# Earlier folds, loaded taps, a finer last batch, and 33 unread products at the start of a fused attention and MLP kernel

## The chip, the cores and the metric

The kernel runs on one core of a Trainium2 chip. The metric is the device time of one execution in microseconds. Before the change it is 587.71 us, the median of three runs (587.62 to 588.37).

## What is computed

Eight batches of attention with packed queries, a gated layer and a gated MLP, all in float32 accuracy. Some weights arrive in float64.

```python
p_packed = sm_attn(p, k, v)              # 32 packed queries per head, 576 keys
out = sm_attn(q, p_packed, p_packed)     # 576 queries, 32 packed keys
x = ...                                  # (8, 576, 512), heads side by side
gate_pre[:, t] = sum over k of conv_w[k] * x[:, t - 4 + k]      # 5 taps
x = (sigmoid(gate_pre) * (x @ w_val)) @ moe_w_out
h = relu(x @ w_in)                       # 512 -> 1024
u, v = h[..., :512], h[..., 512:]
v_n = layer_norm(v)
v_s = einsum('ts,bsd->btd', w_spatial, v_n) + b_spatial
out = (u * v_s) @ moe2_w_out
```

## The kernel before, in words

**Products.** TensorE multiplies in pieces: a matrix is split into a high part (ScalarE, L138) and the rest (VectorE, L140), and a product is the sum of high times high, high times low and low times high. `mm3` and `mms` (L142 to L147) issue these as passes of 288 columns (512 for hv) at L144; nearly all of TensorE's time is there. PSUM tiles come from the pool `ps2`, which has four buffers.

**Setup.** Two of the weight matrices are multiplied once: moe_w_out times w_in gives `wp`, split in high and low parts. `load_raw` (L583) loads a chunk of 128 rows, 64 bits a number; `unit` (L588) decodes it by `from_f64` (L545): two ScalarE passes (L548, L553), a shift (L554) and a sum (L556) on VectorE. `fold` (L594) multiplies: for each of four column blocks m and each half of w_in (u, and v, which the order calls w) four products over k, 128x512 in full float32, two passes each, 32 products in all; then a copy of the high part (L608) and a subtraction (L610), each 128x512. `tap_rows` (L651 to L674) spreads the five convolution taps over the rows in which the first batch wants them: a transpose, a copy, five products with a 0/1 matrix `sel`, a copy. `spatial` and `final` split the two remaining weights.

**Stages of a batch.** `Attn`: sa (scores of p with k by L194, maximum L202 to L214, exponents L219), tr (transposes of these, L229), av (L238, then pp L252), ppt (transpose of pp, L264), sb (scores of q, L273), sn (softmax over them, L286 to L304), sb2 (L306, L311 and the split of the probabilities), m (pp times w_val, L325), cv (gate). Batch 0 alone takes its gate by cx (L360): the taps times pp (ppk, L257) stand in for the convolution. `Mlp`: val (probabilities times m, times the gate), hv (v half, with the layer norm), hu (u half), sp (spatial product; L510 multiplies by u, then g is split by L138 and L140), out (L518 to L537: 48 passes for each of four column blocks, a copy at L535, a store at L537).

**Order.** A string `ORDER` (L21) lists steps, as `0sp2` for the stage sp of tile 2 in batch 0, or `fv1.2` for two steps of a fold; `run` executes the generators in that order, and this fixes the order on each engine's queue. SP issues all loads and stores.

Of the kernel before, what the change touches and what calls it, by code (L numbers as in the profile page):

```python
# [34 lines left out]
0out1 0cv2 0cv0 0out1.2 0cv3 1val2.2 0out3 0cv1 1val1 0out3 0cv0 1val3 1val2 0cv3 1val3 1val2 1val0.3 1val3 1val1.2
0out1 0lk1 0out3 1val2 1val3 1sa0 1val3 1hv2.2 1sa0.3 1tr0 1hv1.2 1hu3.2 1lq1 1hv0 1sa0 1hv1 1tr1 1hv2 1av1 1hv1 1av1
1hu3 0lv0 1hv2 1av0.2 1av1 1hv1.3 2lq0 1av0 1hv2.2 1hu0.2 1lq0 1hv2 1hv0 1hv3 1hv0 1hv4 1hu0 1hv0.2 1hv3 1hv0.2
1ppt0.2 1hv3.2 1hu1 1hv4.3 1sb0 1hv3.2 1hv4 1m0 1sn0 1hv3 1hu1 1sn0.2 1hu1 1hu2.2 1sn1 1m0 1hv4.3 1m0 1hv4.2 1sp0.2
1sn0 1sb20 1sn1.3 1sb21.3 0out0 1sb21 1hu2 1sb20.2 1sp3.2 1lv0 1sb21.2 1sp3.2 1sp2 1sp0.2 1sp3 1sb20.2 1sp1.3 1sb20
1xt0.2 1sp1 1lk1 1sp2 0out3 1sp2.2 1sp0 1xt1.2 1cv0 2val0 1sp1 2val0 1cv3 1sp2 1out2.2 1cv0 1out2.2 1cv2 1cv3 1lv1  # L40
1out0 1out1.2 1cv0 1cv1 1out3 1out0 1cv3 1out1 1out3.2 1cv1 2val0 2val1.2 2val2 1cv2 1cv1 2val1 1lp0 2val2 2val0.2
2val3.2 1cv2 2val2 2val1 1lk0 2val1 1out0.2 2sa0 2val3 2val2.2 2val3 2lq1 2val3 2hv0 2hv3 2hv0 2sa0.2 2hu1.2 2sa0
2hv0.2 2tr0 2sa0 2tr1 2hv3 2hu1 2hv0.2 2hv3 2hv0 2hu0 2hv2 2hv3.2 2av1.2 2hv3 2av0 2hv3 2hv2.3 2av1 2lv1 2av0.2 2hv1
2ppt0 2hv1.2 2ppt0 2hv1 2hu0 2sb0 2hv2 2sn0 2hv4 2hv2.2 2sn1 2hv4.3 2sn0 2hv1.2 2sn1 2hv4.3 2hu0 2hu2.2 2hv4 2sn1 2hv1
2hu2 2hu3.3 2hv4.2 2sp1.2 2sn0.2 2sp1 2sb20 1out1 2sp0.2 2sb20 2sp1 2lv0 2sb20.2 2sp1 2sn1 2sb21.2 2sp2.2 1out3
2sb21.3 2lk1 2sp0.3 2sb20.2 2sp2.2 2lk0 2sp3.3 2sp2 2xt0.2 2sp3.2 2m0.2 2xt1 2sb21 2xt1 2cv0 2m0 2out1 2cv3 2out1 2cv0
2out1 3val2 2cv2 2cv3 2out2 2out0 2cv1 2out2 3val0.2 2out1 2out2.2 2cv1 3val1 2cv2 2cv0 3val0 3lq1 2out0.2 3val2 2cv3
3val1 2cv1 3val1 2out3 2cv2 2out3 3val2 3val3.2 3val0.2 3val1 3sa0 3val3 3val1 3val2.2 3val3 2out3 3lq0 3val3 3hv0.2
3hv1 3sa0.3 3hv1 3hv0.3 3lk1 3hv1.2 3hv3 3sa0 3tr1 3hv4 3hv1.2 3tr0 3hv0.2 3hv1 3hv3 3hv2.2 3av0 3hv3.2 3hv2 3av1
3hu3.2 3hv3.2 3av0.2 3av1.2 3hv3 3ppt0 3hv4.2 3hu3 2out0 3hu1 3hu2 3hv4.2 3ppt0 3sb0 3sn1 3hu2 3hv4 3hv2.2 3hu0 3hv4.2  # L50
3lp0 3hv2 3sn1 3sn0 3hu1 3hu0 3sn1.2 3sn0.2 3hu1 3sn0 3hv2 3hv4.2 3sp1 3hu0 3sp1 3sb21.3 3sp0 3sp2 3sp1.2 3sb20.2 3sp1
3sb21 3lv1 3sp2 3sb21 3hu2 3sp3 3sp0 3sp3 3sb20 3sp2 3sb20.2 3sp2.2 3sp0.2 3xt0 5lp0 3xt0 3sp3.2 3lk0 3sp0 3sb20 3sp3
3m0.2 3xt1 3out0 3xt1 2out3 3out0 3cv0 3cv2 3out0 3out1.2 3sb21 3m0 4val0.2 3cv0.2 4val2 3cv3 3out1 3cv2 3cv1 3out2.2
3out3.2 3out0 3cv3 4val0 3cv3 4val0 4val2 3cv1 4val1.2 3cv2 4val2 3out2 3cv1 4val1 4val2 4val1 3out2 4val0 4val3 4lq1
4val3.3 4val1 4sa0 4val2 4val3 3out3 4hv0.2 4sa0 4hv3 4sa0 4hv3 4hu2.2 4hv4 4hv3 3lv0 4hv3.2 4sa0 4hv0 3out3 4hv3.2
4hv1 4hv0.3 4sa0 4hv0 4hu1 4tr0 4hu1 4hv4.3 4tr1 4av1 4hv1 4av0 4hu2 4hv4.2 4hv2 4hv1.3 4av0 4hv1.2 4av1.2 4av0 4lk0
4hu3 4hu0.2 4lv1 4hu1 4hv2 4hv4.3 4hv2.5 4ppt0 4lq0 4hu0 4ppt0 4hv4 4sp2 4sb0 3out1 4sn0 4sn1 4sn0.2 4hu3.2 4sn1.3
4sp1 4sb21 4sn0 4sb20 4sp2.2 4sp3 4sb21.2 4sp1 4sb20 4sp2 4sp1 4sp0.2 4sb21 4sp3 4sp1 4sp2 4sb20.2 4sb21 4sp0 4lk1
# [22 lines left out]
def packed_attention_gated_mlp(  # L81
# [64 lines left out]
    def mm3(out, steps):  # L146
        mms(out, [p for (ah, al), (bh, bl) in steps for p in ((ah, bh), (ah, bl), (al, bh))])  # L147
# [653 lines left out]
```

## Time and profile before

| what | value |
|---|---|
| median of three runs | 587.71 us (587.62 to 588.37) |
| the profiled execution's own time | 587.61 us |
| its span, first to last instruction | 585.84 us |
| TensorE busy | 570.2 us, 97% |
| VectorE busy | 442.8 us, 76% |
| ScalarE busy | 298.1 us, 51% |
| first product of val | 55.86 us |
| last pass of TensorE | ends at 581.9 us |

The span is 1.77 us shorter than the execution's own time, which also holds what lies around the instructions. TensorE's weight loads (PEld) overlap its passes. A mean granted clock of TensorE of 0.999 stands in the profile, but in the first 18 us it records nothing, and the duration of the weight loads tells the level there.

### The profile page before, as it was taken

How to read it: one execution, taken by the hardware profiler on the slowest of the kernel's cores; microseconds unless marked ns; L12 is line 12 of the kernel's file. 1: busy time of each engine (PE TensorE's matmuls, PEld its weight loads, DVE VectorE, ACT ScalarE, POOL GpSimd, SP SyncE). 2: the span in 40 equal slices, each digit the busy share in tenths (PEclk: the TensorE clock that was granted, in tenths of full speed). 3: DMA queues.
4: the chain of work that ended last, by engine and by line, in shares of the span. 5: the costliest groups of instructions: out<-in, count | busy, mean ns of one | idle time of the engine just before them, and what ended most of it. 6: DMA issues, size and time to landing. Idle time of an engine off the chain costs nothing.

```text
span 585.8 us, 12443 instructions
## 1 busy us (share of the span) xinstructions
PE 570.2 (97%) x5267; PEld 503.1 (86%) x5267; DVE 442.8 (76%) x847; ACT 298.1 (51%) x524; POOL 27.3 (5%) x51
## 2 busy tenths in 40 slices
PE   3998999999999999999999999999999999999997
PEld 2444889898899989898999989898999899998997
DVE  3697899996879867898759866997779968885330
ACT  4678665654435634654436553655446454453321
POOL 2000010000100010001000010001000010001000
PEclk9999999999999999999999999999999999999999
DMA  8965430053203150023300422013500300000012
GB/s 318 409 268 179 152 107 22 1 194 121 62 1 112 62 204 11 21 67 116 97 1 21 168 90 104 19 49 103 190 24 21 102 2 2 1 20 21 1 41 81
DMA packets 16615, 52.55 MB, mean 90 GB/s; under 512 B 1968, under 2 KB 2992, under 8 KB 16560
## 3 DMA queue, kind: packets, MB, share of 16 engines
q1 hardware_dynamic: 16560, 51.77, 25.0%
q8 instruction: 41, 0.67, 0.5%
q14 instruction: 14, 0.11, 0.1%
HBM read 42.32 MB, written 9.44 MB: 88 GB/s over the span
## 4 chain that ended last, share of the span: by engine, by line
PE 93%; DVE 4%; DMA 1%; ACT 1%; issue 0%; SPq 0%; DVEq 0%; ACTq 0%
PE ps L144 82%; PE ps L601 2%; PE ps L238 2%; PE ps L194 2%; PE ps L341 2%; PE ps L273 2%; PE ps L325 1%; DMA kq<-kT 1%; PE ps L360 1%; DVE wp L610 1%; DVE sT L286 0%; DVE sT L306 0%; DVE mx L202 0%; DVE sm L301 0%; DVE raw L556 0%
## 5 line engine op out<-in xcount | busy, mean ns | idle before, releaser
L144 PE MATMUL ps<-ws,vn 128*128 128x288 f32 (+1 forms) x896 | 122.1, 295 | 0.0
L144 PEld LDWEIGHTS ps<-ws,vn 128*128 128x128 f32 (+1 forms) x896 | 119.6, 188 | 2.4 <-issue 1.3
L144 PEld LDWEIGHTS ps<-g,wp 128*128 128x128 f32 x768 | 103.5, 188 | 5.0 <-issue 3.2
L144 PE MATMUL ps<-g,wp 128*128 128x288 f32 x768 | 107.3, 296 | 0.0
L144 PE MATMUL ps<-g,wo 128*128 128x288 f32 x768 | 105.9, 295 | 1.0 <-DVE g L140 1.0
L144 PEld LDWEIGHTS ps<-g,wo 128*128 128x128 f32 x768 | 102.9, 188 | 3.0 <-ACT x L349 1.3
L380 DVE SCALAR_TENSOR_TENSOR acc<-x,cw,acc 128x572 f32<-128x572 f32 (+1 forms) x112 | 90.0, 815 | 4.3 <-ACT acc L376 1.0
L144 PE MATMUL ps<-wp,g 128*128 128x512 f32 x384 | 91.9, 393 | 0.0
L144 PEld LDWEIGHTS ps<-wp,g 128*128 128x128 f32 x384 | 70.8, 188 | 16.5 <-issue 0.7
L138 ACT CAST g<-g 128x576 fp32r<-128x576 f32 x64 | 42.4, 675 | 56.7 <-DVE g L510 40.8
L140 DVE TENSOR_TENSOR g<-g,g 128x576 fp32r<-128x576 f32 x64 | 47.7, 751 | 6.5 <-ACT g L138 5.7
L457 POOL TENSOR_TENSOR rstd<-rstd,mhalf 128x1 f32<-128x1 f32 (+1 forms) x40 | 23.6, 593 | 522.2 <-DVE rstd L455 447.6
L138 ACT CAST vn<-vr 128x512 fp32r<-128x512 f32 (+1 forms) x40 | 24.6, 622 | 45.1 <-DVE vr L459 45.0
L510 DVE TENSOR_TENSOR g<-ps,u 128x576 f32<-128x576 f32 x32 | 23.8, 753 | 27.4 <-PE ps L144 26.9
L535 ACT COPY o<-ps 128x576 f32<-128x576 f32 x32 | 20.3, 635 | 35.7 <-PE ps L144 35.7
L144 PE MATMUL ps<-Ah,Mh 128*128 128x288 f32 x128 | 37.9, 296 | 0.0
L144 PE MATMUL ps<-Ah,Ml 128*128 128x288 f32 x128 | 37.8, 295 | 0.0
L144 PE MATMUL ps<-Al,Mh 128*128 128x288 f32 x128 | 37.8, 295 | 0.0
L439 ACT ACTIVATE vr<-ps 128x512 f32<-128x512 f32 x32 | 19.2, 602 | 34.9 <-PE ps L144 32.3
L140 DVE TENSOR_TENSOR vn<-vr,vn 128x512 fp32r<-128x512 f32 (+1 forms) x40 | 27.0, 684 | 13.1 <-ACT vn L138 12.9
L451 DVE BATCH_NORM_STATS2 st<-vr 128x6 f32<-128x512 f32 (+1 forms) x40 | 27.4, 685 | 11.7 <-ACT vr L439 9.0
L459 DVE TENSOR_SCALAR vr<-vr,mv,rstd 128x512 f32<-128x512 f32 (+1 forms) x40 | 21.2, 536 | 11.9 <-POOL rstd L457 11.8
(108 smaller groups left out, 680.4 us busy)
## 6 DMA issues: line engine op xcount, KB each, us to landing
v<-vT SPq DMA_DIRECT2D x16, 650.0 KB, 5.0
kq<-kT SPq DMA_DIRECT2D x16, 576.0 KB, 4.7
kq<-qT SPq DMA_DIRECT2D x16, 576.0 KB, 4.3
outT<-o SPq DMA_DIRECT2D x32, 288.0 KB, 2.5
raw<-w_in SPq DMA_DIRECT2D x8, 512.0 KB, 10.4
raw<-w_outT SPq DMA_DIRECT2D x4, 512.0 KB, 9.9
raw<-w_val SPq DMA_DIRECT2D x4, 512.0 KB, 10.3
raw<-w_out SPq DMA_DIRECT2D x4, 512.0 KB, 7.6
```

Of the source, the lines that this page charges most:

```text
L138: nc.scalar.copy(out=hi, in_=src)
L140: nc.vector.tensor_tensor(out=lo, in0=src, in1=f32(hi), op=ALU.subtract)
L144: nc.tensor.matmul(out, lhsT=a, rhs=b, start=(i == 0), stop=(i == len(pairs) - 1))
L194: nc.tensor.matmul(ps[g][NPK * qt:NPK * qt + NPK, h // 2, SQ * (h % 2):SQ * (h % 2) + SQ], lhsT=pT_, rhs=k[:, SQ * qt:SQ * qt + SQ], start ...
L238: nc.tensor.matmul(ps[NPK * h:NPK * h + NPK, :65], lhsT=aT[:, 9 * (h // 2) + 4 * (h % 2) + t, :], rhs=v[:, h, t, :], start=(t == 0), stop= ...
L380: nc.vector.scalar_tensor_tensor(out=acc[:, sft:], in0=x[:, :S - sft], scalar=cw[:, c, tap:tap + 1], in1=acc[:, sft:], op0=ALU.mult, op1=A ...
L439: nc.scalar.activation(out=vr, in_=ps, func=AF.Relu)
L451: nc.vector.bn_stats(st[:w], vr[:w])
L457: nc.gpsimd.tensor_tensor(out=rstd[:w], in0=rstd[:w], in1=mhalf[:w], op=ALU.pow)
L459: nc.vector.tensor_scalar(out=vr[:w], in0=vr[:w], scalar1=mv[:w, 0:1], scalar2=rstd[:w], op0=ALU.subtract, op1=ALU.mult,)
L510: nc.vector.tensor_tensor(out=halves(t), in0=ps[:, :, :SH], in1=halves(self.u.pop(c)), op=ALU.mult)
L535: nc.scalar.copy(out=halves(t), in_=ps[:, :, :SH])
```

## The change

- *Taps*: `tap_rows` no longer computes on TensorE. The host repeats the rows (`conv_r`), one load of 128x1280 words brings them, and `from_f64` decodes them in place.
- *Folds*: `fold(j, hf)` makes two column blocks m in one PSUM tile, so that four copies and four subtractions of 128x1024 stand where there were eight and eight of 128x512. The u half comes first.
- *Halves*: the first chunk of w_outT and of w_in are loaded and decoded in two halves; sa yields after two heads, when one tile of k is read; in the last batch hv, hu, sp and out may be interleaved by three passes, and out has a PSUM tile, a copy and a store for each half of 288 columns.
- *Products*: `warm` issues 33 products of the identity with itself (128x128, float32) into one PSUM tile that nothing reads: eight before the first half of sa, six before the second, nineteen before the first fold.
- *Order*: a new `ORDER` for everything.

```diff
+FIRST = ("o0", "w0")
-ik0 ip0 ik1 ic0 cw0.3 cb0 rw0 uw0 sa0 cb0 ro0 sa0 cb0 uw0 uo0.2 rw1 uw1 iv1 cb0 sa0 uw0 uo0 fv3 fv2 sa0 uw1.2 ro1
+ip0 ik0 ik1 ro0 uo0 wm0.8 sa0 wm0.6 sa0.3 uo0 ru0 ro0 uu0.3 uo0 wm0.19 fu0 iv0 ru1 iv1 uo0.3 sa0 tr0 sa0 tr1 fu1 av0.2
...
-    def mms(out, pairs):
-        for i, (a, b) in enumerate(pairs):
-            nc.tensor.matmul(out, lhsT=a, rhs=b, start=(i == 0), stop=(i == len(pairs) - 1))
+    def mms(out, n, pair, cut=False):
+        for i in range(n):
+            a, b = pair(i)
+            nc.tensor.matmul(out, lhsT=a, rhs=b, start=(i == 0), stop=(i == n - 1))
+            if cut and i % 3 == 2 and i < n - 1:
+                yield
...
         def out(self, e):
             ps = ps2.tile([P, 2, 512], F32, tag="ps2", name="ps2")
             cs = slice(P * e, P * e + P)
+            t = f_p.tile([P, S], F32, tag="f", name="o")
+            dst = outT[self.b, e]
             for n in range(2):
+                if self.cut and n:
+                    ps = ps2.tile([P, 2, 512], F32, tag="ps2", name="ps2")
...
+                if self.cut:
+                    nc.scalar.copy(out=t[:, ss], in_=ps[:, n, :SH])
+                    nc.sync.dma_start(out=dst[:, ss], in_=t[:, ss])
+            if not self.cut:
+                nc.scalar.copy(out=halves(t), in_=ps[:, :, :SH])
+                yield
+                nc.sync.dma_start(out=dst, in_=t)
...
     def unit(kind, k):
         raw = raws[kind, k].rearrange("p (n t) -> p n t", t=2)
-        return from_f64(lambda: homes[kind](k), raw, DM, *early)
+        for s in parts(kind, k):
+            yield from from_f64(lambda: homes[kind](k)[:, s], raw[:, s], s.stop - s.start, *early)
+            yield
...
+    def fold(j, hf):
+        ps = ps2.tile([P, 2, 512], F32, tag="ps2", name="ps2")
         hs = slice(hf * DM, (hf + 1) * DM)
         for k in range(NC):
+            for i in range(2):
+                m = 2 * j + i
+                nc.tensor.matmul(
+                    ps[:, i], lhsT=woT[:, k, P * m:P * m + P], rhs=homes["uw"[hf]](k),
+                    start=(k == 0), stop=(k == NC - 1),
+                )
+                yield
...
+        hi, lo = (w[:, 2 * j:2 * j + 2, hs] for w in wp)
+        yield from split(hi, lo, ps)
+
+    def warm(_):
+        ps = ps2.tile([P, 2, 512], F32, tag="ps2", name="ps2")
+        while True:
+            nc.tensor.matmul(ps[:, 0, :P], lhsT=ident, rhs=ident, start=True, stop=True)
+            yield
...
     def tap_rows():
...
+        block = vn_p.tile([P, 4 * n], I32, tag="vn1", name="taps")
+        raw, tmp = block[:, :2 * n].rearrange("p (n t) -> p n t", t=2), block[:, 2 * n:]
+        nc.sync.dma_start(out=raw, in_=words(conv_r))
+        yield
+        dst = block[:, :n]
+        cwr.append(dst.bitcast(F32).rearrange("p (a b) -> p a b", a=CONV))
+        yield from from_f64(lambda: dst, raw, n, tmp=tmp)
```

On TensorE, at the end of the first scores and up to sb, the order before was this (`ps_...` are PSUM tiles, `cw` the taps, `woT` and `winv` or `raw` the two factors of a fold, `aT` the transposed exponents):

```order
L194 MATMUL ps_136<-kq,pbd 32x144
L661 MATMUL ps_169<-ident,cw 20x128
L668 MATMUL ps_194<-cwt,sel 128x128 x5
L601 MATMUL ps_209<-winv,woT 128x512 x2
L601 MATMUL ps_226<-winv,woT 128x512 x2
L601 MATMUL ps_209<-winv,woT 128x512
L238 MATMUL ps_243<-v,aT 32x65 x20
L238 MATMUL ps_266<-v,aT 32x65 x20
L601 MATMUL ps_226<-winv,woT 128x512
L264 MATMUL ps_308<-ident,pp 128x128
```

The same place in the change:

```order
L208 MATMUL ps_134<-kq,pbd 32x144
L628 MATMUL ps_124<-ident 128x128 x19
L615 MATMUL ps_218<-raw,woT 128x512
L615 MATMUL ps_244<-raw,woT 128x512
L253 MATMUL ps_246<-v,aT 32x65 x20
L253 MATMUL ps_273<-v,aT 32x65 x20
L615 MATMUL ps_218<-raw,woT 128x512
L615 MATMUL ps_244<-raw,woT 128x512
L279 MATMUL ps_314<-ident,pp 128x128
L615 MATMUL ps_244<-raw,woT 128x512
```

The taps' six products are gone, nineteen of the unread ones stand in their place, and two folds instead of five stand ahead of av.

On VectorE, between the softmax of batch 0 and the last pieces of setup, the change has these instructions (`sT` are the probabilities of q, `taps` the new decode, `wp` the subtraction of a fold):

```order
L566 ISA raw<-raw,tmp 128x1024
L564 TENSOR_SCALAR taps<-taps 128x640
L322 TENSOR_TENSOR sT<-sT,sm_390 128x576
L566 ISA taps<-taps 128x1280
L564 TENSOR_SCALAR raw<-tmp 128x512
L322 TENSOR_TENSOR sT<-sT,sm_396 128x576
L272 TENSOR_TENSOR ppk<-taps,pp 128x320 x2
L566 ISA raw<-raw,tmp 128x1024
L327 STREAM_TRANSPOSE an<-sT 128x576
L145 TENSOR_TENSOR wp_445<-ps_359,wp_444 128x2x512
L327 STREAM_TRANSPOSE an<-sT 128x576
L145 TENSOR_TENSOR wp_445<-ps_381,wp_444 128x2x512
```

Before, ppk stood ahead of sn, and the subtractions were eight of 128x512 behind both `an`.

On TensorE behind the last sp (`g_...` are the four split products that out reads, the buffer numbers kept), the order before:

```order
L144 MATMUL ps2_6746<-ws1_624,vn1_749 128x288
L144 MATMUL ps2_6811<-g_6763,wo20_805 128x288 x2
L144 MATMUL ps2_6811<-g_6763,wo21_806 128x288
L144 MATMUL ps2_6811<-g_6803,wo20_805 128x288 x2
L144 MATMUL ps2_6811<-g_6803,wo21_806 128x288
```

and in the change, the last rows of a stretch that begins with twenty-four such passes on the other three g:

```order
L150 MATMUL ps2_6861<-g_6838,wo20_672 128x288 x2
L150 MATMUL ps2_6861<-g_6838,wo21_673 128x288
L150 MATMUL ps2_6861<-g_6836,wo20_672 128x288 x2
L150 MATMUL ps2_6861<-g_6836,wo21_673 128x288
L150 MATMUL ps2_6831<-g_6869,wo20_672 128x288 x2
```

Before, g_6803 is first read three passes behind the last sp; now g_6869, the one made last, comes after thirty. On VectorE the last instructions before (`g2_...` is a product with u, `g_...` its low part, `ps2_6746` the last sp) were these:

```order
L140 TENSOR_TENSOR g_6766<-g2_6744,g_6766 128x576
L510 TENSOR_TENSOR g2_6785<-ps2_6729,u_6637 128x576
L510 TENSOR_TENSOR g2_6801<-ps2_6746,u_6586 128x576
L140 TENSOR_TENSOR g_6803<-g2_6785,g_6803 128x576
L140 TENSOR_TENSOR g_6806<-g2_6801,g_6806 128x576
```

and in the change, where `ps2_6730` is the last sp:

```order
L517 TENSOR_TENSOR g2_6802<-ps2_6737,u_6599 128x576
L517 TENSOR_TENSOR g2_6824<-ps2_6675,u_6795 128x576
L145 TENSOR_TENSOR g_6838<-g2_6824,g_6838 128x576
L145 TENSOR_TENSOR g_6836<-g2_6802,g_6836 128x576
L517 TENSOR_TENSOR g2_6845<-ps2_6730,u_6721 128x576
L145 TENSOR_TENSOR g_6869<-g2_6845,g_6869 128x576
```

Before, the low part of g_6803 stood behind the last tile's product with u; now only the last tile's own low part does.

## Rows read from the trace of the kernel before

**Rows 1.** Part 1 of the page: busy time, share of the span and instructions of each engine.
```profile
PE 570.2 (97%) x5267; PEld 503.1 (86%) x5267; DVE 442.8 (76%) x847; ACT 298.1 (51%) x524; POOL 27.3 (5%) x51
```

**Rows 2.** Busy time by stretches: us, each engine's busy time (instructions), granted clock, DMA share, GB/s.
```profile
18.48:55.86 37.38, 35.49 (x349) 15.77 (x347) 29.39 (x60) 26.06 (x47) 0.00 (x0) 1.00 0.70 266
55.86:568.41 512.55, 512.55 (x4755) 469.48 (x4747) 402.89 (x762) 258.34 (x450) 23.62 (x40) 1.00 0.20 69
```

**Rows 3.** TensorE's waits over the span: us in total, times, longest.
```profile
PE ps L194 <- DMA pbd<-pT: 4.9, 1, 4.9
...
PE ps L144 <- DVE g L140: 1.0, 1, 1.0
```

**Rows 4.** TensorE's timeline, 0 to 62 us: start, duration, instruction, idle before.
```profile
4.89 1.22 PE L194 MATMUL ps<-kq,pbd 64*32 64x144 f32 x32 [4.89 <-DMA pbd<-pT]
...
9.91 2.46 PE L668 MATMUL ps<-cwt,sel 20*128 20x128 f32 x10 [0.77 <-ACT cwt L664]
14.04 6.75 PE L601 MATMUL ps<-winv,woT 128*128 128x512 f32 x10 [1.67 <-DVE woT L556]
20.72 1.35 PE L238 MATMUL ps<-v,aT 128*32 128x65 f32 x80
...
24.27 1.20 PE L273 MATMUL ps<-kq,ppT 64*32 64x288 f32 x32
...
39.51 5.31 PE L601 MATMUL ps<-raw,woT 128*128 128x512 f32 x12
46.67 1.12 PE L601 MATMUL ps<-raw,woT 128*128 128x512 f32 x2 [1.85 <-DVE wp L610]
47.72 2.68 PE L360 MATMUL ps<-an,ppk 32*64 32x288 f32 x80
```

**Rows 5.** Timeline of TensorE's weight loads, 13 to 22 us.
```profile
17.62 0.34 PEld L601 LDWEIGHTS ps<-winv,woT 128*128 128x128 f32 x1 [0.52 <-issue]
18.47 0.20 PEld L601 LDWEIGHTS ps<-winv,woT 128*128 128x128 f32 x1 [0.52 <-issue]
18.91 0.19 PEld L601 LDWEIGHTS ps<-winv,woT 128*128 128x128 f32 x1 [0.24 <-issue]
```

**Rows 6.** ScalarE's timeline, 6 to 18 us: the first exponents.
```profile
12.69 1.20 ACT L219 ACTIVATE a<-ps,nb 128x144 f32<-128x144 f32 x4 [0.52 <-DVE nb L214]
```

**Rows 7.** Groups by line and form, 0 to 62 us: busy us, mean ns of one, idle before.
```profile
L610 DVE TENSOR_TENSOR wp<-ps,wp 128x512 fp32r<-128x512 f32 x8 | 5.3, 683 | 1.6 <-ACT wp L608 1.6
...
L556 DVE CUSTOM_DVE_ANT_0 raw<-raw,tmp 128x1024 uint16<-128x1024 uint16 x4 | 2.7, 684 | 0.0
...
L369 ACT ACTIVATE gate<-ps 128x288 f32<-128x288 f32 x8 | 2.6, 422 | 0.0
...
L554 DVE TENSOR_SCALAR raw<-tmp 128x512 int32<-128x512 int32 x4 | 1.7, 415 | 0.5 <-ACT tmp L553 0.5
...
L301 DVE TENSOR_REDUCE sm<-sT 128x18 f32<-128x576 f32 x2 | 1.4, 721 | 0.0
...
L140 DVE TENSOR_TENSOR Ml<-ps,Mh 128x1024 fp32r<-128x1024 f32 x1 | 1.2, 1225 | 2.5 <-ACT Mh L138 2.5
L325 PE MATMUL ps<-wval,ppT 64*32 64x512 f32 x16 | 1.1, 601 | 0.0
```

**Rows 8.** Timeline, 567 to 586 us.
```profile
567.92 0.76 DVE L510 TENSOR_TENSOR g<-ps,u 128x576 f32<-128x576 f32 x1 [1.11 <-PE ps L144]
568.60 1.58 DVE L140 TENSOR_TENSOR g<-g,g 128x576 fp32r<-128x576 f32 x2
...
569.40 12.50 PE L144 MATMUL ps<-g,wo 128*128 128x288 f32 x92 [0.99 <-DVE g L140]
...
582.00 0.64 ACT L535 COPY o<-ps 128x576 f32<-128x576 f32 x1 [0.96 <-PE ps L144]
```

**Rows 9.** DMA traffic, 2 to 38 us.
```profile
DMA packets 4152, 14.11 MB, mean 392 GB/s; under 512 B 582, under 2 KB 838, under 8 KB 4149
```

**Rows 10.** DMA issues, 560 to 586 us: KB each, median us from issue to landing.
```profile
outT<-o SPq DMA_DIRECT2D x6, 288.0 KB, 2.1
```

More of the change, by code (lines that the diff above doesn't have):

```diff
@@ L140, in split, with mm3, pair @@
         nc.vector.tensor_tensor(out=lo, in0=src, in1=f32(hi), op=ALU.subtract)
-    def mms(out, pairs):
-        for i, (a, b) in enumerate(pairs):
-            nc.tensor.matmul(out, lhsT=a, rhs=b, start=(i == 0), stop=(i == len(pairs) - 1))
-    def mm3(out, steps):
-        mms(out, [p for (ah, al), (bh, bl) in steps for p in ((ah, bh), (ah, bl), (al, bh))])
+    def mms(out, n, pair, cut=False):
[4 more added lines that the diff above has]
+                yield
+    def mm3(out, n, step, cut=False):
+        def pair(i):
+            (ah, al), (bh, bl) = step(i // 3)
+            return ((ah, bh), (ah, bl), (al, bh))[i % 3]
+        return mms(out, 3 * n, pair, cut)
     vn = []
@@ L179, in __init__, with scores, head @@
             self.pp = self.ppk = self.x = None
-        def heads(self, lhsT, kind):
-            src = [kq_t.pop((kind, self.b, i)) for i in range(2)]
-            return [ps2.tile([P, 2, 512], F32, tag="ps2", name="ps2") for _ in range(2)], [
-                (g, h, lhsT[64 * g:64 * g + 64, NPK * h:NPK * h + NPK], src[h // 2][64 * g:64 * g + 64, h % 2])
-                for h in range(4)
+        def scores(self):
+            return [ps2.tile([P, 2, 512], F32, tag="ps2", name="ps2") for _ in range(2)]
+        def head(self, lhsT, kind, h):
+            src = kq_t[kind, self.b, h // 2]
+            return [
+                (g, lhsT[64 * g:64 * g + 64, NPK * h:NPK * h + NPK], src[64 * g:64 * g + 64, h % 2])
                 for g in range(2)
@@ L189, in sa @@
         def sa(self, _):
-            ps, heads = self.heads(pbd_t.pop(self.b), "k")
-            for i in range(0, 8, 2):
+            ps = self.scores()
+            for h in range(4):
                 for qt in range(4):
-                    for g, h, pT_, k in heads[i:i + 2]:
+                    for g, pT_, k in self.head(pbd_t[self.b], "k", h):
                         nc.tensor.matmul(
@@ L269, in sb @@
         def sb(self, _):
[L270 removed]
+            ps = self.scores()
             for n in range(2):
[L272 to L277 removed]
+                for h in range(4):
+                    for g, pT_, q in self.head(self.ppT, "q", h):
+                        nc.tensor.matmul(
+                            ps[g][NPK * h:NPK * h + NPK, n, :SH],
+                            lhsT=pT_, rhs=q[:, n * SH:(n + 1) * SH],
+                            start=True, stop=True, tile_position=(64 * g, NPK * h),
+                        )
             self.sps = ps
@@ L400, in val @@
                 ss = slice(n * SH, (n + 1) * SH)
[L401 to L406 removed]
+                yield from mm3(
+                    ps[:, n, :SH], 2,
+                    lambda g: ((at.M[0][:, g, cs], at.M[1][:, g, cs]), (at.A[g][0][:, ss], at.A[g][1][:, ss])),
                 )
@@ L440, in hv @@
             else:
-                mms(ps, [(self.tail[:, k, :], wk) for k in range(NC) for wk in (w_hi[k], w_lo[k])])
+                yield from mms(ps, 2 * NC, lambda i: (self.tail[:, i // 2, :], (w_hi, w_lo)[i % 2][i // 2]))
                 yield
@@ L770, in by_pair @@
         return np.moveaxis(w, 0, axis)
+    conv = rows(by_pair(inputs["moe_conv_w"].T, 0)).transpose(1, 0, 2)
     wt, bias = inputs["moe2_w_spatial"].T, inputs["moe2_b_spatial"]
```

250 lines of the change are left out of this document (100 added, 150 removed).

## The prediction

> **What bounds the kernel now.** I read the views in this order. The page says that TensorE is busy for 97% of the span and VectorE for 76% [rows 1], but a share mixes stages, so the table of stretches comes next [rows 2]. From 55.86 to 568.41 us TensorE is busy 512.55 of 512.55 us: only fewer passes could shorten that stretch, and the change takes none away there. What an edit of order can win lies ahead of 55.86, where the first product of val starts, and behind 568.41. TensorE's waits, six in all, say how much: 4.9 us for p is the first, 1.0 for a g the last [rows 3], and the larger ones between are 1.7 for woT and 1.85 for a wp [rows 4]. Last come the timelines of the two ends [rows 4 to 8]. In front, S, the end of L273's products, is 25.47 us (24.27 + 1.20), and from there the chain of waits runs over VectorE up to the fold that starts at 46.67. Behind, TensorE ends at 581.9, and one copy and one store close the span at 585.84.
>
> The sum is made against the profiled execution, whose own time is 587.61. It is 0.1 us (0.02%) under the median of the three runs, 587.71, so nothing is added for that.
>
> **Taps.** The transpose, the wait for its copy (0.77 us) and the five products (2.46 us in ten passes [rows 4]) leave TensorE between 8.75 and 12.37; two ScalarE copies go too. Behind them the first fold waited 1.67 us for woT anyway [rows 4], so by itself their going saves nothing. In their place stand one load of 655 KB and one decode. The load is the 22nd on SP's queue; one chunk of w_in and all of w_val wait behind it, 1.7 us at the 392 GB/s of this stretch [rows 9], and are read long after they land. The decode adds a shift and a sum on VectorE, about 0.4 and 0.75 us from start to start, being 640 wide where the others are 512. Its two ScalarE passes stand against the two copies.
>
> **Up to S.** Before, five fold products (ten passes, 6.75 us) stand between the taps and av. Their weight loads are 0.34 us long and 0.85 apart for two passes until 17.62, and 0.20 long and 0.43 apart from 18.47 [rows 5]: the lower level of TensorE's clock (1.2 GHz), then the higher (2.4), after 4.4 us of folds without a gap. In the change two fold products stand ahead of av and three more before sb. Worked forward: p and the first k land near 5.0 as before, and the scores of two heads take 1.2; the second k lands near 7.4; the scores end at T = 9.3 (8.82 before). From T to the first exponent before took 3.9 us (to 12.69 [rows 6]) with two shifts of a decode in it; without them 3.2. Behind nb VectorE has the shifts and sums of half of woT and of the first u, 1.65 us: the first fold can start at 14.15. Two folds take 1.7 us at the higher clock; exponents (1.2 us a half [rows 6]) and transposes are done at 15.6 and 16.35, so av (1.35) ends at 17.2; two folds, 18.9; pp is ready at 19.05, ppt ends at 19.4, one fold at 20.3, sb at S = 21.5, 4.0 us earlier.
>
> **From S to val.** TensorE has 27 fold products left at 0.86 us (twelve passes in 5.31 us, two to a product [rows 4]), 23.2 us; cx takes 2 x 2.68 and m 1.09 [rows 4, 7]: 29.6 us. VectorE's list from sn's first transpose to Ml, each at the distance at which its kind follows another: 12 shifts at 0.34 and 12 sums at 0.60 (busy 0.42 and 0.68 [rows 7], overlapping), half a sum 0.35, the taps' 1.15, the softmax 9.0 (twelve wide instructions at about 0.7, as L301, and small ones), ppk 0.95, three subtractions of wp and Ml at 1.2, two of Al at 0.67: 29.0 us. A subtraction for two m at once costs 1225 ns where two single ones cost 2 x 683 = 1366 [rows 7], so 0.14 us goes for each pair. The two engines are even, and neither can hide the other's gaps. Before, VectorE waited 1.6 us for ScalarE's copies ahead of the eight L610 [rows 7]; for four I allow 0.7 us, since a copy is twice as wide. First val at S + 30.3 = 51.8 instead of 55.86: **-4.1 us.** Bounds: without gaps 51.1 (-4.8); with twice the allowance 52.5, and with another wait like TensorE's 1.85 on a wp [rows 4] 53.4 (-2.5).
>
> **The 33 products.** They are 66 passes in TensorE's queue, ahead of work that cannot pass them: eight products in the wait for p, six between the halves of the scores, nineteen in the wait for the first woT and u. The nearest row is L668 [rows 4]: ten passes of 128 columns, 0.21 us from start to start (2.46 less the last pass's own length), at the lower clock; 0.107 at the higher. The eight take 3.4 us from about 1.5 and are done near 5.0: hidden. The six take 1.3 or 2.6 us from 6.4, to between 7.7 and 9.0, against k at 7.4; that is the 0.5 us in T. The nineteen take 4.1 or 8.1 us against the 4.85 from T to the first fold: hidden at the higher clock, 3.3 over at the lower. Before, the clock rose 4.4 us after folds without a gap began; here TensorE works almost without one from 1.5 on, so I take the higher clock for the nineteen, and nothing beyond T. With the cover gone, the 66 would cost between 7.1 and 14.1 us. What they return is already in S: at the lower clock the first two folds would take 3.4 us instead of 1.7, and av would start at 17.6 instead of 16.35.
>
> **The middle.** From the first val to the last sp the same passes stand in another order, 0.136 us each whichever stage they are of (92 in 12.50 [rows 8]). Zero, with 0 to +1.0 as bounds (one more wait as long as the tail's).
>
> **The tail.** Before, out reads g_6803 after three passes. Its low part (the first L140 of [rows 8]) stands on VectorE behind the last tile's L510, which could start only when the last sp was done (567.92): hence TensorE's wait of 0.99 [rows 8]. Now the low parts of three g stand ahead of the last L517, and the first product on the fourth g comes thirty passes, 4.1 us, behind the last sp. Its chain, one L145 still ahead of it, is four steps of at most 0.79 us, near 2.7 (ScalarE's split is priced as VectorE's): **-1.0 us**, bounds 0 and -1.0. The last copy is 288 columns wide: 0.42 (as L369 [rows 7]) for 0.64 [rows 8], -0.2. The last store has 147 KB for 295. From issue to landing a store takes 2.1 us [rows 10], of which 0.75 are data at 392 GB/s [rows 9]; half of the data is -0.38, the bounds are 0 and -1.05. I take -0.35, since the transfer is the part that surely scales: **-0.55 us** with the copy. The Trainium skill, page "DMA: Bandwidth & Descriptors", section "Bandwidth", says that small transfers run far below the full rate and gives 0.95 us for 64 KB and 6.15 for 1 MB; an estimate between the two is 2.16 us for 288 KB, as the trace has it, and 1.38 for 144, by which the sum would be 581.6.
>
> **Sum:** 587.61 - 4.1 - 1.0 - 0.55 = 581.96, say **582.0 us**, 1.0% faster.
>
> **Rivals.** *VectorE sets the front (0.18).* The fold at 46.67 waits for it already [rows 4], and it gets the taps' 1.15 us more. If its list meets the waits of before again, val starts at 53.4 to 54.6: 583.5 to 584.7. For: the two lists are within 0.6 us of each other. Against: pairs save 0.6 us, and it starts 4 us earlier.
>
> *The front gives nothing (0.06).* If loads set its end, an earlier S would not help, since 14.1 MB at 392 GB/s land near 38 us either way, and the loads ahead of the last units set the rest. Only the tail is left: 586.1. Against: TensorE's waits from 9.9 us on name engines [rows 4].
>
> *The products overrun (0.06), the side of slower.* TensorE works in order, so the first fold starts when the nineteen end. The point is 19.9 us: a start 4.1 us behind 14.15 (18.25) eats the front's gain, 1.6 more the tail's. If the clock stays low until the folds, T is 10.2, the nineteen end at 18.3, and the folds after them lose 2.2 us more: val at 57.9, 588.1, 0.1% slower. If a pass takes the 0.34 us of its cold weight load [rows 5], the nineteen alone take 12.9 us, and the time is about 596, 1.4% slower. For: no row of before shows the clock so early. Against: 0.21 is a measured distance, and the products begin 12 us before the folds of before.
>
> **How the numbers follow.** The main case (0.70) is 580.8 to 583.4; the range reaches up over VectorE's case and down by the store's other bound: 580.4 to 585.2 holds about 0.82. A measurement tells 0.2%, 1.2 us, from no change, so faster is below 586.5: main, VectorE's case and a third of the case without the front, 0.90. The same: the rest of that case and the mildest overrun, 0.05. Slower: the other overruns, 0.05.
>
> **What would show it.** Right: the nineteen end before 14.2, weight loads of the first folds are 0.20 long, sb ends near 21.5, the first val starts near 51.8, no g stands among TensorE's waits at the end, the last copy lasts 0.42. Wrong: a wait of TensorE on VectorE of over 1.5 us between 25 and 50; weight loads of 0.34 behind the nineteen; a wait in the middle stretch; or a first val before 50.5, which would mean that I have overrated VectorE's list.

## The result, and the profile after

The changed kernel takes 581.98 us (median of four runs, 581.48 to 583.02) where the kernel before takes 587.66 beside it: a ratio of 0.9904 with a 95% interval of 0.9887 to 0.9921. The prediction said 582.0. The profiled execution took 581.8 us, with a span of 579.94; before it was 587.61 with 585.84, so the span fell by 5.90.

Part 1 of the page of the change, which answers to [rows 1]:

```profile
PE 574.3 (99%) x5322; PEld 509.8 (88%) x5322; DVE 445.1 (77%) x849; ACT 299.8 (52%) x528; POOL 27.2 (5%) x49
```

TensorE is busy for longer than before, 574.3 against 570.2 us, in a shorter span: the unread products are in it. The table of stretches of the change, cut at S (the end of sb), at the first val, at the first pass of out and at the last pass (as in [rows 2]: length, then each engine's busy time, granted clock, DMA share, GB/s):

```profile
0.00:21.39 21.39, 19.26 (x254) 13.89 (x254) 9.44 (x29) 10.40 (x25) 0.70 (x6) 1.00 0.91 347
21.39:51.26 29.87, 29.87 (x232) 14.06 (x231) 29.18 (x56) 26.44 (x45) 1.56 (x3) 1.00 0.93 359
51.26:563.83 512.57, 512.30 (x4748) 469.21 (x4744) 404.44 (x763) 259.07 (x452) 24.98 (x40) 1.00 0.19 66
563.83:576.72 12.89, 12.88 (x98) 12.64 (x96) 2.07 (x3) 3.47 (x8) 0.00 (x0) 1.00 0.20 70
576.72:579.94 3.22, 0.00 (x0) 0.00 (x0) 0.00 (x0) 0.40 (x1) 0.00 (x0) 1.00 0.28 92
```

| step | before | change | difference |
|---|---|---|---|
| S | 25.47 | 21.39 | -4.08 |
| S to the first val | 30.39 | 29.87 | -0.52 |
| first val to TensorE's last pass | 526.04 | 525.45 | -0.59 |
| last pass to the end of the span | 3.93 | 3.23 | -0.70 |

From S to the first val TensorE is busy all the time, and VectorE for 29.18 of 29.87 us. TensorE's waits over the whole span, all that the view lists (for [rows 3]):

```profile
PE ps L628 <- POOL ident masks.py:199: 1.4, 1, 1.4
PE ps L615 <- DVE woT L566: 0.5, 1, 0.5
PE ps L208 <- DMA kq<-kT: 0.2, 1, 0.2
```

None is for a g, for the taps or for a wp. TensorE's timeline of the first 54 us (start, duration, instruction, idle before), which answers to [rows 4]:

```profile
1.35 3.78 PE L628 MATMUL ps<-ident 128*128 128x128 f32 x16 [1.35 <-POOL ident masks.py:199]
5.29 1.22 PE L208 MATMUL ps<-kq,pbd 64*32 64x144 f32 x32 [0.15 <-DMA kq<-kT]
6.43 1.62 PE L628 MATMUL ps<-ident 128*128 128x128 f32 x12
7.98 0.72 PE L208 MATMUL ps<-kq,pbd 64*32 64x144 f32 x32
8.64 4.51 PE L628 MATMUL ps<-ident 128*128 128x128 f32 x38
13.67 1.98 PE L615 MATMUL ps<-raw,woT 128*128 128x512 f32 x4 [0.52 <-DVE woT L566]
15.58 1.36 PE L253 MATMUL ps<-v,aT 128*32 128x65 f32 x80
16.87 1.98 PE L615 MATMUL ps<-raw,woT 128*128 128x512 f32 x4
...
20.19 1.20 PE L289 MATMUL ps<-kq,ppT 64*32 64x288 f32 x32
21.32 2.84 PE L615 MATMUL ps<-raw,woT 128*128 128x512 f32 x6
24.00 13.90 PE L615 MATMUL ps<-winv,woT 128*128 128x512 f32 x32
37.74 5.31 PE L615 MATMUL ps<-raw,woT 128*128 128x512 f32 x12
```

The nineteen products end at 13.15 us and the first fold waits 0.52 us more for VectorE, so they are hidden. Sixteen passes of the first eight take 3.78 us, the thirty-eight passes of the nineteen 4.51, half as much a pass: TensorE was at its higher clock by then. The two halves of the scores show the change of level too, 1.22 us and 0.72. At the other end, the timeline of the last 3 us and the stores of the last 20 (KB each, median us to landing), for [rows 8] and [rows 10]:

```profile
576.74 0.40 ACT L541 COPY o<-ps 128x288 f32<-128x288 f32 x1 [0.40 <-PE ps L150]
```

```profile
outT<-o SPq DMA_DIRECT2D x8, 144.0 KB, 1.8
```

### The profile page after: what moved, and what is told of

Read it like the earlier page. It is cut to its first block, busy times and chain, and to the rows that moved or that the text cites. A ratio compares the mean times of both kernels' runs of the same rounds, so it can differ in the third digit from the quotient of the medians.

```text
span 579.9 us, 12567 instructions
## 1 busy us (share of the span) xinstructions
PE 574.3 (99%) x5322; PEld 509.8 (88%) x5322; DVE 445.1 (77%) x849; ACT 299.8 (52%) x528; POOL 27.2 (5%) x49
## 4 chain that ended last, share of the span: by engine, by line
PE 94%; DVE 3%; DMA 1%; ACT 1%; issue 0%; POOL 0%; SPq 0%; POOLq 0%; ACTq 0%
PE ps L150 81%; PE ps L615 5%; PE ps L208 2%; PE ps L357 2%; PE ps L253 2%; PE ps L289 1%; PE ps L341 1%; PE ps L376 1%; DMA kq<-kT 1%; DVE vn L145 0%; DVE st L466 0%; PE ps L628 0%; DVE vr L474 0%; DVE sT L307 0%; DVE sT L302 0%
## 5 line engine op out<-in xcount | busy, mean ns | idle before, releaser
L150 PEld LDWEIGHTS ps<-g,wp 128*128 128x128 f32 x768 | 105.2, 188 | 5.1 <-issue 2.8
L150 PE MATMUL ps<-g,wp 128*128 128x288 f32 x768 | 109.4, 296 | 0.0
L150 PE MATMUL ps<-wp,g 128*128 128x512 f32 x384 | 93.7, 394 | 0.0
L472 POOL TENSOR_TENSOR rstd<-rstd,mhalf 128x1 f32<-128x1 f32 (+1 forms) x40 | 25.0, 627 | 481.9 <-DVE rstd L470 419.9
L499 ACT ACTIVATE u<-ps 128x576 f32<-128x576 f32 x32 | 20.7, 650 | 22.3 <-PE ps L150 22.1
```

The lines of the kernel that those rows point to most:

```text
L150: nc.tensor.matmul(out, lhsT=a, rhs=b, start=(i == 0), stop=(i == n - 1))
L472: nc.gpsimd.tensor_tensor(out=rstd[:w], in0=rstd[:w], in1=mhalf[:w], op=ALU.pow)
L499: nc.scalar.activation(out=halves(u), in_=ps[:, :, :SH], func=AF.Relu)
```

## Experiments

All twelve compare with runs of the kernel before on the same chip (medians 587.25 to 587.29 us). "Span" and the times of single steps are those of the profiled execution.

### What do the 33 products bring?

The first group takes parts of them away, or doubles them, by the tokens of the order alone.

```diff
-ip0 ik0 ik1 ro0 uo0 wm0.8 sa0 wm0.6 sa0.3 uo0 ru0 ro0 uu0.3 uo0 wm0.19 fu0
+ip0 ik0 ik1 ro0 uo0 sa0 sa0.3 uo0 ru0 ro0 uu0.3 uo0 fu0
```

This is the first run, without any of them; the others differ in the same tokens.

> The changed kernel without its 33 products; everything else as it is. Theory A (the products pay by the clock): the second tile of k lands at 6.6 us, so the scores end near 8.0 instead of 8.7 and VectorE has the first fold's factors near 12.9; but the weight loads of the first folds are 0.34 us long, two folds take 3.4 us instead of 2.0, and S (end of the products of sb) is 0.5 to 1.2 us later than 21.4: about 582.5 to 583.2 where the change has 582.0. Theory B (they only fill waits, and the six even delay the scores): S is earlier by up to 0.4 us, and the time is 581.6 to 582.0.

> Only the nineteen products ahead of the first fold are left out, so TensorE has nothing from 8.7 us to the first fold near 13.6. Theory A (the clock falls back in such a gap): weight loads of the first folds are 0.34 us long, two folds take 3.4 us, S is 0.5 to 1.2 us later: 582.5 to 583.2. Theory B (it stays up): weight loads of 0.19, S within 0.1 us, 582.0.

> 66 products instead of 33 (16, 12 and 38). Their cover is gone: by passes of 0.21 us up to about 5.9 us and 0.118 behind, the products end near 20.4 us, 6.7 us behind the change's first fold. Theory A (TensorE's order decides from there): first fold, S and the first val move by 6.5 to 6.9 us, and the time is about 588.6. Theory B (VectorE sets the front, and catches up while TensorE is held): VectorE is ahead with its decodes, so the first val moves by only 4 to 5 us: 586 to 587.

> Only the six products between the halves of the scores are left out. The second tile of k landed at 6.57 us in the change, and the second half of the scores started at 7.98, behind these six. Theory A (they delay VectorE's chain): the second half starts near 6.6, the scores end 1.0 to 1.4 us earlier, the first fold starts near 12.5; S comes only 0.2 to 0.4 us earlier, because the last tile of q lands at 19.8 and sb takes 1.2: about 581.7. Theory B (the clock would not be up without them): scores at 1.2 us a half instead of 0.72 and folds with weight loads of 0.34: no gain or 0.5 to 1 us slower.

| kernel | median, us | ratio to before (95%) | S | first val | span |
|---|---|---|---|---|---|
| the change | 581.98 | 0.9904 (0.9887 to 0.9921) | 21.39 | 51.26 | 579.94 |
| without all 33 | 582.75 | 0.9927 (0.9915 to 0.9940) | 22.69 | 52.53 | 580.97 |
| without the nineteen | 583.55 | 0.9938 (0.9926 to 0.9951) | 23.17 | 53.05 | 581.66 |
| without the six | 581.45 | 0.9900 (0.9885 to 0.9915) | 21.14 | 51.00 | 579.58 |
| 66 products | 587.99 | 1.0013 (1.0004 to 1.0022) | 28.37 | 58.25 | 586.85 |

**Without all 33** the timeline of TensorE reads:

```profile
5.21 2.54 PE L208 MATMUL ps<-kq,pbd 64*32 64x144 f32 x64 [5.21 <-DMA kq<-kT]
12.71 3.78 PE L615 MATMUL ps<-raw,woT 128*128 128x512 f32 x4 [4.96 <-DVE woT L566]
16.42 1.76 PE L253 MATMUL ps<-v,aT 128*32 128x65 f32 x80
```

The first fold starts 0.96 us earlier than in the change, as Theory A had it (12.9), but its four passes take 3.78 instead of 1.98 us and av 1.76 instead of 1.36, and S is 1.30 us later. So the products return 0.8 us of the median (1.0 of the span), and through the clock. The two intervals of the ratio overlap by a little, so the reading rests on these steps of the timeline; the change's own profile, taken a second time, has S at 21.54 and the first val at 51.43, far less apart from the first one than the 1.3 us here.

**Without the nineteen** is the slowest of these but for the doubling. Its stretches from 9 us to the first fold, to the end of av and to 22:

```profile
9.00:13.13 4.13, 0.00 (x1) 0.01 (x1) 3.88 (x16) 3.52 (x11) 0.00 (x0) 0.79 1.02 420
13.13:18.77 5.64, 5.64 (x85) 3.01 (x85) 2.44 (x7) 1.82 (x6) 0.00 (x0) 0.55 1.04 412
18.77:22.00 3.23, 3.23 (x18) 1.14 (x13) 2.29 (x7) 2.57 (x8) 0.00 (x0) 1.00 1.01 401
```

The clock had risen: the second half of its scores took 0.72 us. TensorE then did nothing for 5.0 us, and the granted clock is a mean of 0.79 there and of 0.55 while the first folds and av run, near the lower of the two levels (1.2 of 2.4 GHz). Two folds took 3.78 us and av 2.00:

```profile
13.13 3.78 PE L615 MATMUL ps<-raw,woT 128*128 128x512 f32 x4 [4.95 <-DVE woT L566]
16.84 2.00 PE L253 MATMUL ps<-v,aT 128*32 128x65 f32 x80
```

So Theory A holds for the gap, at a larger price than expected (1.6 us of the median against 0.5 to 1.2), and fourteen products alone are worse than none: they delay the first fold by 0.42 us (13.13 against 12.71), and the folds find the clock low all the same.

**66 products** move the first fold from 13.67 to 20.74 us, S by 6.98 and the first val by 6.99. Nothing is caught up behind, as Theory A said; the 66 added passes cost 0.106 us each on balance. That is less than they take: from start to start a pass of the last 76 takes 0.113 us (12.15 to 20.74), and of the first 32 with the lower clock among them 0.21 (1.35 to 7.97). Against that, the added passes fill the 0.52 us in which the change's first fold waits, and the first half of the scores takes 0.72 us behind them instead of 1.22. Here is the overrun that the prediction had as its rival, made by hand: one doubling takes the whole gain of the change.

**Without the six** the second half of the scores waits for k itself and starts at 6.56 us instead of 7.98. The first fold comes 1.43 us earlier, but then TensorE waits for v and for pp:

```profile
6.56 0.72 PE L208 MATMUL ps<-kq,pbd 64*32 64x144 f32 x32 [0.61 <-DMA kq<-kT]
7.21 4.51 PE L628 MATMUL ps<-ident 128*128 128x128 f32 x38
12.24 1.99 PE L615 MATMUL ps<-raw,woT 128*128 128x512 f32 x4 [0.52 <-DVE woT L566]
14.15 0.78 PE L253 MATMUL ps<-v,aT 128*32 128x65 f32 x40
15.63 0.78 PE L253 MATMUL ps<-v,aT 128*32 128x65 f32 x40 [0.69 <-DMA v<-vT]
```

and S is only 0.25 us earlier. The load of v (0.69 us of waiting) and pp (0.38 ahead of ppt) bound this front next. The pair was run once more:

> The changed kernel as it is, once more, beside the three below on the same chip: 582.0, first val near 51.3.

> The changed kernel without the six products, once more, beside the change itself. If the gain of the first run of it was real, 0.2 to 0.5 us less than the change in the same call, and the first val near 51.0; if it lay in the spread between runs, no difference.

The change took 581.79 (ratio 0.9907, 0.9891 to 0.9923), the kernel without the six 581.44 (0.9903, 0.9889 to 0.9917). The medians without the six are lower both times, by 0.5 us (in runs that did not stand side by side) and by 0.35, and the intervals overlap widely. In the second profile av waited 1.2 us for v, S was 21.91 and the first val 51.79, where the change's second profile has 51.43, and the span was longer, 580.36 against 579.95. So whether it gains is open; by the medians it is at most 0.1%.

### Is VectorE's list as long as TensorE's?

```diff
         yield from from_f64(lambda: dst, raw, n, tmp=tmp)
+        c, t = tmp[:, :n], tmp[:, n:2 * n]
+        nc.vector.tensor_scalar(dst, c, 3, None, op0=ALU.logical_shift_left)
+        nc.vector.tensor_tensor(out=dst, in0=dst, in1=t, op=ALU.add)
```

> The taps' shift and sum on VectorE are done twice over (same result), 1.15 us more of its list between S and the first val. Theory A (TensorE sets the front from S to val, as the chain of waits of the change reads: its folds follow one another from 21.4 to 43.0 without a wait): VectorE has slack there, first val within 0.3 us of 51.3, 582.0 to 582.3. Theory B (the two lists are even, as the prediction had it): +0.8 to +1.15 us, 582.8 to 583.2.

It took 582.58 us (ratio 0.9923, 0.9909 to 0.9936). S is the same (21.34), the first val 52.22 instead of 51.26. From the start of the second pair (L680, L681) to the next instruction VectorE needs 1.27 us:

```profile
36.31 0.49 DVE L680 TENSOR_SCALAR taps<-taps 128x640 int32<-128x640 int32 x1
36.84 0.82 DVE L681 CUSTOM_DVE_ANT_0 taps<-taps 128x1280 uint16<-128x1280 uint16 x1
37.58 0.42 DVE L564 TENSOR_SCALAR raw<-tmp 128x512 int32<-128x512 int32 x1
```

and that next one starts 1.38 us later than in the change:

```profile
36.20 0.42 DVE L564 TENSOR_SCALAR raw<-tmp 128x512 int32<-128x512 int32 x1
```

Of these 1.3 to 1.4 us the first val loses 0.96. TensorE's waits are the change's and some new ones, among them these two, for VectorE:

```profile
PE ps L615 <- DVE raw L566: 0.6, 1, 0.6
...
PE ps L341 <- DVE wp L145: 0.3, 1, 0.3
```

Theory B holds: the chain of waits of the change runs over TensorE alone from S on, but VectorE has only 0.3 to 0.4 us of slack. Of two even engines the chain here named one.

### The halves at the start

```diff
-FIRST = ("o0", "w0")
+FIRST = ()
```

with the tokens of the second halves taken out of the order.

> The first chunk of w_outT and that of w_in are loaded and decoded whole again (256-column halves gone at the start only). Theory A (the first fold waits for VectorE's list behind nb): that list is 0.34 + 0.34 + 0.6 + 0.6 us instead of 1.65 with half a chunk, so the first fold starts 0.3 us later, S 0 to 0.3, 582.0 to 582.4. Theory B (the loads decide: u lands 0.65 us later and ScalarE decodes 0.4 us more ahead of the first fold): first fold and S 0.6 to 1.1 us later, 582.6 to 583.1.

It took 582.37 us (ratio 0.9916, 0.9901 to 0.9930), with the first fold at 14.36 instead of 13.67, S at 22.09 and the first val at 51.95: +0.7 on each. TensorE's wait for woT is 0.9 us instead of 0.5. In this execution the scores ended 0.3 us later than in the profile of the change, so about 0.4 belong to the halves and 0.3 to the spread of that; that lies between the theories.

No run takes back the loaded taps, the folds in pairs or the new order of the front by itself. What the timelines say is this. Without the products S is at 22.69, 2.78 us earlier than before: the first fold starts at 12.71 instead of 14.04, and five fold products instead of seven stand ahead of sb. Behind S the change owes those two (1.7 us at the higher clock) and still needs 0.52 us less than before, mainly because the wait of 1.85 us on a wp [rows 4] is gone. How the 2.78 us are shared among taps, halves and order is not shown by a run, but for the 0.4 to 0.7 of the halves.

### The tail

```diff
-                if self.cut and n:
-                    ps = ps2.tile([P, 2, 512], F32, tag="ps2", name="ps2")
...
-                if self.cut:
-                    nc.scalar.copy(out=t[:, ss], in_=ps[:, n, :SH])
-                    nc.sync.dma_start(out=dst[:, ss], in_=t[:, ss])
+                if self.cut and n:
+                    nc.scalar.copy(out=halves(t), in_=ps[:, :, :SH])
+                    nc.sync.dma_start(out=dst, in_=t)
```

> The changed kernel with the last batch's out copied and stored whole again: one PSUM tile, one copy of 576 columns and one store of 288 KB for each column block; the order of TensorE's passes stays that of the change. From the last pass to the end of the span the change has 3.23 us, the kernel before 3.93. Theory A (the halves are worth what copy and transfer shrink by): 3.9 us again, +0.7, about 582.7 where the change has 582.0. Theory B (a store's time is mostly fixed): only the copy's 0.24 come back, 582.2.

It took 582.97 us (ratio 0.9926, 0.9914 to 0.9939). From the last pass to the end it has 3.75 us against 3.23: +0.52, of which the copy is 0.24 (0.64 for 0.40) and the store 0.28. (The median rose by 1.0; in the profile the first val is 0.18 later as well, which the edit does not touch.) The stores of its last stretch take, from issue to landing:

```profile
outT<-o SPq DMA_DIRECT2D x4, 288.0 KB, 2.1
```

where those of half the size took 1.8. The result lies between the theories: halving 288 KB saves 0.3 us of 2.1. The whole tiles end 3.75 us behind the last pass, and not 3.93 as before, so the halves are 0.52 of the 0.70 us that this end gained; the cause of the other 0.18 stays open, and one profile (without the halves at the start) has 3.06 for the change's own end. In this run TensorE waits for no g, so the wait that went is not owed to the halves of out.

> The changed kernel up to the last batch, and for the last batch's hv, hu, sp and out the order and the whole tiles, copies and stores of the kernel before. Theory A (three steps add up): the wait of about 1.0 us on a g returns behind the last sp and the 3.9 us behind the last pass too, together +1.7: 583.7 where the change has 582.0, and the first val stays near 51.3. Theory B (the finer order of the last batch gives more, in hv and hu too, or less): over 584.2, or under 583.0.

Its edit sets `self.cut` to False and puts the last batch's tokens of before in place of those of the change. It took 584.22 us (ratio 0.9948, 0.9934 to 0.9963). The wait is back, in the timeline:

```profile
564.19 0.76 DVE L514 TENSOR_TENSOR g<-ps,u 128x576 f32<-128x576 f32 x1 [1.11 <-PE ps L147]
564.86 1.58 DVE L142 TENSOR_TENSOR g<-g,g 128x576 fp32r<-128x576 f32 x2
...
565.66 12.51 PE L147 MATMUL ps<-g,wo 128*128 128x288 f32 x92 [0.99 <-DVE g L142]
```

These are [rows 8] again, under other line numbers. The first val stays at 51.25, and the last pass comes 526.92 us behind it instead of 525.45, so the order of the last batch is worth 1.47 us: 0.99 are the wait, and by the starts of the passes some 0.35 arise in the last hv and hu, which the change interleaves more finely; the rest lies around the wait. With 0.54 behind the last pass the tail is worth 2.0 us of the span, over Theory A's 1.7; the median, 2.24 us above the change's, lies at the edge of Theory B. The run also measures the middle. With the last batch ordered alike in both, the stretch from the first val to the last pass is 526.92 us here and 526.04 before. So the new order of the other batches costs 0.88 us, and by the starts of the passes most of it lies in hv, whose 384 passes take 90.04 us where they took 89.08.

> Without the six products, and the very last copy (288 columns) shared: ScalarE takes 144 columns and VectorE the other 144, with one store behind both. Theory A (copy and store stand in a row at the end): the copy is over in 0.25 to 0.3 us instead of 0.40, the tail is 3.1 instead of 3.23 us, and the time is 0.1 to 0.15 below the kernel without the six. Theory B (the store's start waits for two engines, which costs as much): no difference.

It took 581.41 us (ratio 0.9901, 0.9888 to 0.9914), no difference to the kernel without the six. The two copies did not run side by side:

```profile
576.27 0.28 ACT L542 COPY o<-ps 128x144 f32<-128x144 f32 x1 [0.40 <-PE ps L150]
576.58 0.31 DVE L543 COPY o<-ps 128x144 f32<-128x144 f32 x1 [10.41 <-ACT o L542]
```

VectorE waited for ScalarE's copy into the same tile, and the tail is 3.38 us, 0.15 longer than the change's, as the copy is 0.2 longer. So this profile agrees with copy and store standing in a row, and doesn't say what a true split would give; that wasn't tried.

### The products alone, on the kernel before

The kernel before gets the change's `warm` and its tokens, and nothing else:

```diff
-... rw0 uw0 sa0 cb0 ro0 sa0 cb0 uw0 uo0.2 rw1 uw1 iv1 cb0 sa0 uw0 uo0 fv3 fv2
+... rw0 uw0 wm0.8 sa0 cb0 ro0 sa0 cb0 uw0 uo0.2 rw1 uw1 iv1 cb0 sa0 uw0 uo0 wm0.8 fv3 fv2
```

> The kernel before, with nothing of the change but sixteen of the products: eight ahead of the first scores, eight ahead of the first fold. Theory A (a cold first stretch costs the kernel before as well, and S sets VectorE's chain): weight loads at the first folds are 0.19 us long, the first ten fold passes take 4.4 us instead of 6.75, S is 2.0 to 2.4 us earlier and the time 585.0 to 585.5 where before has 587.3. Theory B (VectorE bounds that front with its own work): S is earlier, but the fold at 46.67 is not, and the time stays within 0.4 us of before. Theory C (the 1.5 us wait for the second tile of k keeps the clock low): weight loads of 0.34 at the first fold, and 0.3 to 1.5 us slower.

The median of twelve runs is 588.81 us against 587.29 (ratio 1.0013, 0.9997 to 1.0028), but the runs lie in three groups: two at 585.1 and 585.3, two at 587.1 and 587.5, eight from 588.8 to 589.2, with mean granted clocks of 0.999, 0.994, and 0.990 to 0.991. Only the last kind has a profile. Its stretches, and the lines of TensorE that matter:

```profile
9.00:16.90 7.90, 7.19 (x28) 6.06 (x29) 6.80 (x19) 7.28 (x18) 0.00 (x0) 0.57 1.02 414
16.90:47.00 30.10, 28.18 (x171) 12.16 (x170) 24.10 (x52) 19.91 (x38) 0.00 (x0) 1.00 0.75 295
47.00:52.00 5.00, 5.00 (x83) 2.80 (x82) 4.83 (x10) 3.33 (x6) 0.00 (x0) 0.66 0.32 76
```

```profile
9.71 2.07 PE L674 MATMUL ps<-cwt,sel 20*128 20x128 f32 x10 [1.20 <-ACT cwt L670]
11.71 3.78 PE L615 MATMUL ps<-ident 128*128 128x128 f32 x16
15.28 5.30 PE L601 MATMUL ps<-winv,woT 128*128 128x512 f32 x10
46.49 1.12 PE L601 MATMUL ps<-raw,woT 128*128 128x512 f32 x2 [1.88 <-DVE wp L610]
47.54 4.37 PE L360 MATMUL ps<-an,ppk 32*64 32x288 f32 x80
```

The clock had risen by the second half of the scores (0.73 us). Then TensorE did one transpose and waited 1.2 us for its copy, and the clock was low for most of the time from 9 to 16.9 us (a mean of 0.57). The second eight products ran at it, 3.78 us, and held the first fold back to 15.28 (14.04 before). S was 25.27, 0.2 us earlier than before's 25.47. Theory C has the weight loads (0.34 us at 16.14) and the time right, and the cause wrong: the clock was up behind the second tile of k, and fell after the taps' transpose. Behind the wait of 1.88 us for a wp the clock fell a second time, and the first cx took 4.37 us where before has 2.68 [rows 4] behind the same wait. The fastest two runs fit Theory A's 585.0 to 585.5. The two stretches explain the granted clocks of the groups by an estimate: 0.43 of 7.90 us are 0.0058 of 587, and 0.34 of 5.00 are 0.0029, so a run with both has 0.991, one with the first alone 0.994, one with neither 1.0. That fits the three groups and their times, as the low cx alone is 1.7 us; the runs of the two faster groups have no profile that would show it.

## Why the prediction was right, step by step

**Up to S** (21.5 forecast, 21.39 measured): right, by errors that cancel in part. The scores ended at 8.7 us, not 9.3: their second half started at 7.98, about where it was worked out, but took 0.72 us instead of 1.2, as the clock was up. (The second k landed by 6.6 and not at 7.4, as the run without the six shows; here the half stood behind the six anyway.) The first fold started at 13.67 (14.15 forecast), 5.0 us behind the scores where 4.85 were worked out. The half us was lost again ahead of ppt, which started at 18.96 (19.05 forecast). TensorE was busy until 18.85, since two folds take 1.91 us from start to start (13.67 to 15.58) and not 1.7, and this twice. And pp, for which ppt waits, was ready no earlier than 18.9: the chain of waits of the change runs there over VectorE's L264, the shift and sum of a decode (L564, L566), and L264 and L265 again. The run without the six shows the same with a larger lead: 1.43 us became 0.25, since av then waits for v and ppt for pp.

**S to the first val** (30.3 and 29.87; first val 51.8 and 51.26): right in both lists, 29.6 for TensorE and 29.0 for VectorE, against 29.87 and 29.18 busy. The 0.7 us allowed for VectorE's waits on ScalarE were too much: VectorE waited 0.4 us for Mh and nothing for a wp. TensorE's own list was 0.27 longer than worked out and had no gap, so it set the stretch. That the engines are even, on which the step rested, is shown by the doubled taps. Two slips in the forecast touch no term of its sum: 0.85 us is the distance of single passes of a fold, not of two (the sums use it so), and a wait of 1.85 us would end at 53.65, not 53.4.

**The 33 products**: hidden at the higher clock, as forecast, and their price without cover came out at 7.0 us for 66 passes, the 7.1 of the prediction, in part by luck: the added passes take more, and a filled wait and faster scores give some of it back. What they return was called part of S and put at 1.2 us through av; without them S is 1.3 us later. That this agrees is luck too. The two cold folds cost 1.80 us more, as forecast (1.7), but the forecast let av wait for the transposes when the folds are quick, which took 0.5 us off, and left out what the run shows: av itself is 0.40 us slower at the lower clock, and the first fold starts 0.96 us earlier without the products.

**The middle** (0, bounds 0 and +1.0): in bounds, but not 0 and near the upper one. From the first val to the last pass the change has 0.59 us less than before. The run with the old tail divides this: the order of the last batch gives 1.47 and the new order of the others costs 0.88. Of that 0.27 are idle, as the table of stretches shows (512.30 us busy in 512.57). The rest are passes that follow one another at longer distances, most of them in hv. The forecast's step that the same passes cost the same in any order, 0.136 us each whichever stage they are of, is what failed here; a pass of hv, 512 columns wide, takes 0.23. Why the order matters to them stays open.

**The tail**: the wait of 0.99 is gone with the order, as forecast, and that order gave 1.47 in all where 1.0 was forecast. The copy was 0.40 (0.42 forecast). The store was over-priced by a little: 0.35 forecast, 0.28 measured by the whole store. Behind the last pass 0.70 us went, 0.55 forecast; 0.52 of them are copy and store. An estimate between the rows of the table in the Trainium skill (page "DMA: Bandwidth & Descriptors", section "Bandwidth"), which is of loads from HBM to SBUF, is 2.16 us for 288 KB and 1.38 for 144. The trace of these stores agrees with the larger one (2.1) and not with the smaller, which took 1.8.

**The sum.** Span: -4.08 - 0.52 - 0.59 - 0.70 = -5.9; forecast -4.1 - 1.0 - 0.55 = -5.65. The front gave 0.5 us more than forecast, and middle and tail together 0.25 less: in the middle +0.88 for 0, in the tail -2.2 for -1.55. That the median met 582.0 to 0.02 us is luck, with such errors in the terms and runs from 581.48 to 583.02. Of the rivals, the one on VectorE had the right place but the engine was 0.3 to 0.4 us short of deciding; the one on an overrun is real at twice the number of products.

## What to carry to other kernels

Work that nobody reads pays only if it ends in work: products up to the first real product kept TensorE's higher clock and returned 1 us, fourteen of them followed by 5 us of nothing cost more than none, and twice as many took the whole gain. Count the passes against the wait that they fill, at the measured price a pass, and look at the weight loads or granted clock of the first real product. Where one engine's chain has no wait left, measure how far the next engine is behind before counting on another gain: here it was 0.3 to 0.4 us. At the end, let only the last tile's own steps stand behind the last product, and give TensorE other products meanwhile: that removed a wait of 1 us. And do not price a new order of the same passes at nothing: here it cost 0.9 us that no wait in the list showed.

## What was not expected of the hardware

- The moment at which the clock rises differs between executions of one program. The kernel without the six has 0.72 us for the first half of the scores in its first profile and 1.22 in its second. With the same eight products ahead, it took 1.22 us in the change's profile and 0.72 in those without the nineteen and with the taps twice. This moves the end of the scores by some 0.5 us. S need not follow: with the taps twice the scores ended 0.5 us earlier than in the change, and S is 21.34 against 21.39.
- In the products put alone on the kernel before, the time has three levels some 2 us apart (585.2, 587.3, 588.9) on one chip, and the granted clock differs with them (0.999, 0.994, 0.991). The kernel before, whose weight loads are long up to 17.6 us [rows 5], lay between 586.2 and 588.3 beside it, without such groups.
- Half of a store's bytes save 0.3 of its 2.1 us (medians of eight and of four stores; with the old tail four whole ones have 2.3).
